# RWKV scan and expert router: a chunk's 96 rows on partitions 16 to 111, one transfer where there were two

## The chip, the core and the metric

The kernel runs on one core of a Trainium2 chip. The metric is the time of one execution in device microseconds, as the median of several runs. The profile that is shown is one execution under the hardware profiler.

## The reference, cut to what matters

Two parts follow one another. The first is a linear recurrence for each of 4 batches and 8 heads over 768 tokens of width 48. The second sends every token with a positive score through one of 8 experts.

```
state = 0                                     # 48 x 48 per batch and head
for t in range(768):
    cur = outer(u * k[t], v[t])
    y[t] = r[t] @ (state + cur)
    state = w[t][:, None] * state + outer(k[t], v[t])
x = y, laid out as 3072 tokens of 384
out = x
for the tokens with x @ w_skip > 0:
    e = argmax(x @ w_gate)
    out = x + prob[e] * (relu(x @ w1[e]) @ w2[e])
```

## The kernel before

The recurrence is done in 24 chunks of 128 tokens (4 batches of 6 chunks). A chunk's r, k and w lie in one SBUF tile `wrk`, its v transposed in a tile `vt`, and v with the tokens on the partitions in a tile `v`. A partition of `wrk` and `vt` is one of the 48 elements of one head; the four pairs of heads (`NP` = 4) lie side by side along the row. The first head of a pair has partitions 0 to 47, the second 64 to 111, and the rows from 48 to 63 and from 112 on are zeros, set once. `wrk` has three buffers, `vt` four, `v` four.

For every chunk the work goes through these steps. `products` (POOL) multiplies neighbouring decays into `p` (L281), makes `rk` = r * k (L283; for chunk 0 VectorE does it) and changes half of r and k in place (L290). `prep_scan`, `prep_keys` and `prep_reads` run the scans on VectorE (L297, L315), make `kq` on POOL (L313) and `rp` on VectorE (L320). `scores` (TensorE, L338) writes the two score matrices of a pair to `psA`, `mask` (VectorE, L354) makes `asb` of them, `keys` transposes `kq` (L347), `bonus_sums` (L363) and `bonus` (VectorE, L367) start `psY`. One step later `update` (L376) adds k-transposed times v to the state `psu`, `outputs` (L403, L408) adds the masked scores and the old state to `psY`, and `rows_out` (L421) turns the result into rows of tokens and router logits. A chunk of a batch's end has no `update`, so there are 20 of them. Three chunks are in flight at a time: while TensorE is at chunk s for `update` and `outputs`, it is at s + 1 for `scores`, and POOL is at s + 3 for `products`.

The order of the instructions on each engine is the order in which this code is written (`manual_schedule`). The loads of a chunk are issued on SP four steps ahead, by `load_chunk` (L154 for r, k, w, L156 for vt) and `load_v` (L161). Chunk 0 alone comes from an array `wrk0` whose gaps are already filled with zeros on the host, in whole transfers of 128 partitions, on SP and on ACT's queue (L146 to L151).

One more thing sets when a transfer is issued. The framework gives the transfers of SP and ACT, in order, to eight semaphores, DMAHW0 to DMAHW7, in turn. A transfer that takes a semaphore which is in use waits on its queue until the transfer that had it before has landed, and what stands behind it on that queue waits too.

At the end of the recurrence the tokens are gathered by expert, and the experts run one after the other; that part is not touched by the change.

Of the kernel before, what the change touches and what calls it, by code (L numbers as in the profile page):

```python
# [8 lines left out]
F32 = mybir.dt.float32  # L9
# [17 lines left out]
NP = H // 2  # L27
# [14 lines left out]
R_OFF = 1 + NP * CW  # L42
K_OFF = R_OFF + NP * P
V_OFF = K_OFF + NP * P
HP = 64
LO = HP + D
XW = 2 * D + E + 1
X2 = XW + 2 * D
BIG = 65536.0
# [2 lines left out]
C_ID, C_TRI, C_IOTA, C_TOK, C_DESC, C_HS = 0, 128, 256, 512, 560, 608  # L52
# [5 lines left out]
def rwkv_moe_kernel(ctx, tc, wrk, wrk0, vN, uP, wgs, wgp, w12, cst, out):  # L58
    nc = tc.nc
    dram = ctx.enter_context(tc.tile_pool(name="dram", bufs=1, space=bass.MemoryType.DRAM))  # L60
    yd = dram.tile([DM, NT], F32, name="yd")

    keep = ctx.enter_context(tc.tile_pool(name="keep", bufs=1))
# [70 lines left out]
    with tc.tile_pool(name="att", bufs=2) as att, \  # L134
# [1 line left out]
        NBUF = 3  # L136
        wrk_sb = [pers.tile([P, V_OFF], F32, name=f"wrk{i}") for i in range(NBUF)]
        vt_sb = [pers.tile([P, NP, P], F32, name=f"vt{i}") for i in range(NBUF + 1)]
        v_sb = {}

        def load_chunk(i):
            b, c = seq[i]
            t = wrk_sb[i % NBUF]
            vf = vt_sb[i % (NBUF + 1)].rearrange("p a j -> p (a j)")
            if i == 0:
                nc.sync.dma_start(t[:, :R_OFF], wrk0[:, :R_OFF])  # L146
                nc.scalar.dma_start(t[:, K_OFF:V_OFF], wrk0[:, K_OFF:V_OFF])
                nc.sync.dma_start(t[:, R_OFF:K_OFF], wrk0[:, R_OFF:K_OFF])
                nc.scalar.dma_start(c_sb[:, :C_IOTA], cst[:, :C_IOTA])
                nc.sync.dma_start(u_sb, uP)  # L150
                nc.scalar.dma_start(vf, wrk0[:, V_OFF:V_OFF + NP * P])  # L151
                return
            for g in range(2):
                nc.sync.dma_start(t[64 * g:64 * g + D], wrk[b, c, g, :, :V_OFF])  # L154
            for g in range(2):
                nc.sync.dma_start(vf[64 * g:64 * g + D], wrk[b, c, g, :, V_OFF:V_OFF + NP * P])  # L156

        def load_v(i):
            b, c = seq[i]
            v_sb[i] = att.tile([P, H, D], F32, tag="v", name=f"v{i}", bufs=4)  # L160
            nc.sync.dma_start(v_sb[i], vN[b, c])  # L161

        bias_lo = keep.tile([P, 1], F32, name="bias_lo")
        bias_hi = keep.tile([P, 1], F32, name="bias_hi")
# [9 lines left out]
        identb = keep.tile([P, P], BF16, name="identb")  # L174
        tok = c_sb[:, C_TOK:C_TOK + 2 * B * NC].rearrange("p (c q) -> p c q", q=2)
        desc = c_sb[:, C_DESC:C_DESC + NC * E].rearrange("p (c e) -> p c e", e=E)
        rows1 = c_sb[:, C_HS + 2:C_HS + 3]
        rows1_ = c_sb[:, C_HS + 3:C_HS + 4]
        wgp_sb = keep.tile([P, NP, XW], F32, name="wgp_sb")
        wgs_sb = keep.tile([P, KC, E + 1], F32, name="wgs_sb")  # L180
# [6 lines left out]
        psu = psr[:, :NP * HP].rearrange("p (a j) -> p a j", a=NP)  # L187
        psy = ps1.tile([P, NP, P], F32, tag="psY", name="psY")
        psa = [ps1.tile([P, NP, P], F32, tag=f"psA{g}", name=f"psA{g}") for g in range(2)]
        sblk = [pers.tile([P, NP, 2, HP], F32, name=f"sblk{i}") for i in range(2)]  # L190
        ohs = keep.tile([P, 1, E], BF16, name="ohs")
        key = keep.tile([P, NC, E + 1], F32, name="key")
        rall = keep.tile([P, B * NC, 1], F32, name="rall")
# [25 lines left out]

        def setup():  # L220
            load_chunk(0)
            load_v(0)
            nc.gpsimd.memset(warm, 0.0)
            nc.vector.memset(bias_lo, W_LO)
            nc.vector.memset(wrk_sb[1], 0.0)
            nc.vector.memset(bias_hi, -Q_MAX)
            nc.vector.memset(smaskb, Q_MIN)
            nc.vector.memset(smaskb.rearrange("p (a j) -> p a j", a=NP)[:, :, 0:1], 1.0)
            nc.vector.tensor_copy(pss[:, :NP * HW // 2], smaskb.bitcast(F32))
            for g in range(2):  # L230
# [38 lines left out]
        work, lgs, gens = {}, {}, {}  # L269
# [99 lines left out]
        def update(i):  # L369
            b, c = seq[i]  # L370
            if c == NC - 1:
                nc.vector.memset(psu, 0.0)
                return
            for a in range(NP):
                for g in range(2):
                    nc.tensor.matmul(psu[64 * g:64 * g + D, a, :D],  # L376
                                     work[i]["kt"][:, a, 64 * g:64 * g + D],
                                     v_sb[i][:, 2 * a + g, :D],
                                     start=False, stop=True, skip_group_check=True)

        def carry(i):
# [7 lines left out]
        def carry_out(i):  # L389
            b, c = seq[i]  # L390
            if c == NC - 1:
                return
            nb = sblk[(i + 1) % 2]
            for g in range(2):
                rows = slice(64 * g, 64 * g + HP)
                nc.scalar.copy(nb[rows, :, g, :D], psu[rows, :, :D])

        def outputs(i):
            b, c = seq[i]
            wk, v = work[i], v_sb.pop(i)  # L400
# [198 lines left out]

        with tc.manual_schedule():  # L600
            setup()
            fill(FILL0)
            products(0)
            for s in range(-2, n + 1):
                on = lambda i: 0 <= i < n
                if s + 4 < n:
                    load_chunk(s + 4)
                if on(s + 3) and s + 3 >= 1:
                    load_v(s + 3)
                if s == -2:  # L610
# [14 lines left out]
                if on(s):  # L625
                    update(s)
# [3 lines left out]
                if on(s):  # L630
                    outputs(s)
# [20 lines left out]
                if on(s):  # L652
                    carry_out(s)
# [177 lines left out]

    rv = nc.values_load(flag_i[0:1, 0:1], min_val=0, max_val=2)
    with tc.If(rv > 0):
        general_path(tc, wrk, w12, yd, u_sb, c_sb, wgs_sb, out)


def general_path(tc, wrk, w12, yd, u_sb, c_sb, wgs_sb, out):
    nc = tc.nc
    ident = c_sb[:, C_ID:C_ID + P]
    desc = c_sb[:, C_DESC:C_DESC + E]  # L840
# [2 lines left out]
    with tc.tile_pool(name="ga", bufs=1) as ga, tc.tile_pool(name="gp", bufs=2, space=PSUM) as gp:  # L843
        rt = ga.tile([P, S], F32, name="g_r")
        kt = ga.tile([P, S], F32, name="g_k")
# [35 lines left out]
    with tc.tile_pool(name="gm", bufs=1) as gm, tc.tile_pool(name="gq", bufs=1, space=PSUM) as gq:  # L881
        with tc.For_i(0, NT, P) as t0:
# [28 lines left out]
            for e in range(E):  # L911
# [77 lines left out]
```

## Time and profile before

| what | value |
|---|---|
| median of 3 runs | 312.46 us (312.44 to 315.95) |
| the profiled execution: time | 312.3 us |
| the profiled execution: span | 310.5 us |
| TensorE busy | 290.5 us (94%) |
| POOL busy | 161.5 us (52%), nearly all of it in the first 140 us |
| VectorE busy | 225.2 us (73%) |
| ScalarE busy | 153.3 us (49%) |
| bytes moved | 60.44 MB, mean 195 GB/s |

The time of an execution is its span and some 1.8 us around it. An instruction's line is that of the kernel before, as L376. "PEld" is TensorE's loading of weights, which has rows of its own and may lie beside matmuls. A float32 matmul is recorded as two instructions, so the 8 matmuls of an `update` are 16 rows. "DMA share" is the time of the packets as a share of what 16 DMA engines have; it can pass 1, since an engine may have more than one packet under way. "To landing" is the time from the start of a transfer's issue until its semaphore tells that it is there.

### The profile page before, as it was taken

What the parts mean: (1) busy time and instruction counts of PE and PEld (TensorE: products, weight loads), DVE (VectorE), ACT (ScalarE), POOL (GpSimd) and SP (SyncE); (2) the same over time, 40 slices, a digit from 0 to 9 for tenths busy, and PEclk for the clock granted to TensorE, in tenths of its full rate; (3) what the DMA queues carried; (4) which work ended last, traced back from release to release, by engine and by line L of the source; (5) the groups of instructions that cost most, each with busy time, mean ns of one, the idle gap of its engine ahead of it and who ended that gap; (6) DMA issues with size and microseconds to landing.
All of it is one profiled execution on the core that took longest, in us unless ns stands there. A gap on an engine that the chain in (4) does not pass through costs nothing.

```text
span 310.5 us, 8353 instructions
## 1 busy us (share of the span) xinstructions
PE 290.5 (94%) x3229; PEld 270.9 (87%) x3229; DVE 225.2 (73%) x486; ACT 153.3 (49%) x408; POOL 161.5 (52%) x160
## 2 busy tenths in 40 slices
PE   6589999899999999899999999999999999999990
PEld 2479898798898979789888999999999999999990
DVE  5567777999989999998553778594967859495310
ACT  3234465566356556546332648281846648282300
POOL 9897889898889999877004412221212222201111
PEclk9759999999999999999999999999999999999997
DMA  7999999999999999985111396747386774720000
GB/s 228 212 228 245 204 257 270 280 245 245 240 282 253 250 260 222 231 221 163 53 51 54 96 364 242 265 128 288 135 266 232 244 255 153 264 88 25 8 28 14
DMA packets 23777, 60.44 MB, mean 195 GB/s; under 512 B 4902, under 2 KB 11338, under 8 KB 23728
## 3 DMA queue, kind: packets, MB, share of 16 engines
q1 hardware_dynamic: 21248, 53.69, 64.0%
q0 software_dynamic: 2048, 5.48, 5.4%
q8 instruction: 27, 0.44, 0.7%
q10 hardware_dynamic: 432, 0.66, 0.6%
q14 instruction: 22, 0.18, 0.2%
HBM read 52.76 MB, written 7.86 MB: 195 GB/s over the span
## 4 chain that ended last, share of the span: by engine, by line
PE 81%; DMA 7%; DVE 6%; issue 2%; POOL 1%; ACT 1%; POOLq 0%; SPq 0%; DVEq 0%
PE psY L403 7%; PE psY L408 7%; PE psA L338 7%; PE psO L805 7%; PE psO L807 7%; PE psO L806 7%; PE psH L784 6%; PE psH L783 6%; PE psH L782 6%; PE psB L363 6%; DMA wrk<-wrk 5%; PE psX L421 5%; PE psT L347 3%; DVE asb L354 2%; PE psu L376 2%
## 5 line engine op out<-in xcount | busy, mean ns | idle before, releaser
L746 POOL DMA_INDIRECT out<-fin,ids x16 | 17.1, 1070 | 76.7 <-DVE fin L812 36.0
L789 ACT ACTIVATE hh<-psH 128x256 fp32r<-128x256 f32 x60 | 23.1, 384 | 57.1 <-PE psH L784 53.9
L784 PE MATMUL psH<-xTh,w1l 128*128 128x256 f32 x168 | 47.5, 283 | 0.0
L783 PE MATMUL psH<-xTl,w1h 128*128 128x256 f32 x168 | 47.5, 283 | 0.0
L782 PE MATMUL psH<-xTh,w1h 128*128 128x256 f32 x168 | 47.5, 283 | 0.0
L684 POOL DMA_INDIRECT xg<-out,idr x15 | 16.1, 1071 | 48.0 <-DMA out<-fin,ids 26.7
L805 PE MATMUL psO<-w2h,hh 128*128 128x384 f32 x120 | 40.7, 339 | 0.0
L807 PE MATMUL psO<-w2h,hl 128*128 128x384 f32 x120 | 40.1, 334 | 0.0
L806 PE MATMUL psO<-w2l,hh 128*128 128x384 f32 x120 | 40.1, 334 | 0.0
L290 POOL TENSOR_TENSOR wrk<-wrk 128x512 f32<-128x512 f32 x24 | 36.2, 1508 | 1.8
L413 ACT COPY xT<-psY 128x512 f32<-128x512 f32 x24 | 14.1, 586 | 45.6 <-PE psY L408 34.5
L354 DVE TENSOR_TENSOR asb<-psA,c_sb 128x512 f32<-128x512 f32 x48 | 30.7, 680 | 7.8 <-PE psA L338 7.8
L790 DVE SCALAR_TENSOR_TENSOR hl<-psH,hh 128x256 fp32r<-128x256 f32 x60 | 25.2, 420 | 12.5 <-ACT hh L789 12.1
L313 POOL TENSOR_TENSOR kq<-wrk,q 128x512 f32<-128x512 f32 x24 | 26.9, 1119 | 13.6 <-DVE q L297 12.1
L784 PEld LDWEIGHTS psH<-xTh,w1l 128*128 128x128 f32 x168 | 32.2, 192 | 0.0
L783 PEld LDWEIGHTS psH<-xTl,w1h 128*128 128x128 f32 x168 | 32.2, 192 | 0.0
L782 PEld LDWEIGHTS psH<-xTh,w1h 128*128 128x128 f32 x168 | 32.2, 191 | 0.0
L403 PE MATMUL psY<-asb,v 128*48 128x128 f32 x384 | 26.4, 281 | 5.4 <-DVE psY L367 5.3
L338 PE MATMUL psA<-rp,kq 64*64 64x128 f32 (+1 forms) x768 | 27.9, 265 | 3.1 <-POOL kq L313 3.1
L812 DVE SCALAR_TENSOR_TENSOR fin<-psO,gates,xg 128x384 f32<-128x384 f32 x15 | 9.3, 618 | 28.5 <-PE psO L807 28.5
L283 POOL TENSOR_TENSOR rk<-wrk 128x512 f32<-128x512 f32 x23 | 29.5, 1282 | 0.0
L97 DVE TENSOR_TENSOR w2l<-r,w2h 128x512 fp32r<-128x512 f32 x42 | 27.8, 687 | 1.0
(143 smaller groups left out, 680.2 us busy)
## 6 DMA issues: line engine op xcount, KB each, us to landing
r<-w SPq DMA_DIRECT2D x48, 512.0 KB, 6.0
wrk<-wrk SPq DMA_DIRECT2D x46, 288.9 KB, 7.1
v<-vN SPq DMA_DIRECT2D x24, 192.0 KB, 5.8
out<-x SPq DMA_DIRECT2D x24, 192.0 KB, 5.4
vt<-wrk SPq DMA_DIRECT2D x46, 96.0 KB, 6.1
wrk<-wrk SPq DMA_DIRECT2D x1, 258.5 KB, 3.9
wrk<-wrk ACTq DMA_DIRECT2D x1, 256.0 KB, 4.1
wrk<-wrk SPq DMA_DIRECT2D x1, 256.0 KB, 4.5
```

What stands on the lines that cost most here:

```text
L97: (eng or nc.vector).tensor_tensor(dst_l, src, dst_h.bitcast(F32), op=ALU.subtract)
L283: (nc.gpsimd if i else nc.vector).tensor_tensor(rk.rearrange("p a j -> p (a j)"), t[:, R_OFF:K_OFF], t[:, K_OFF:V_OFF], op=ALU.mult)
L290: nc.gpsimd.tensor_tensor(rk1, rk1, two(1, 1, CW), op=ALU.mult)
L338: nc.tensor.matmul(psa[g][j:j + HP, a, j:], wk["kq"][rows, a, j:j + HP], wk["rp"][rows, a, j:], start=True, stop=True)
L354: nc.vector.tensor_tensor(s, psa[g], tri.rearrange("p (o j) -> p o j", o=1).to_broadcast([P, NP, P]), op=ALU.mult)
L403: nc.tensor.matmul(psy[64 * g:64 * g + D, a], v[:, 2 * a + g], wk["asb"][g][:, a], start=False, stop=(c == 0), skip_group_check=True)
L782: nc.tensor.matmul(ps, w1h[:, o:o + P], xTh[:, kc], start=(kc == 0), stop=False)
L783: nc.tensor.matmul(ps, w1h[:, o:o + P], xTl[:, kc], start=False, stop=False)
L784: nc.tensor.matmul(ps, w1l[:, o:o + P], xTh[:, kc], start=False, stop=(kc == KC - 1))
L805: nc.tensor.matmul(pso, h[j, fc][0], w2h[:, o], start=(fc == 0), stop=False)
L806: nc.tensor.matmul(pso, h[j, fc][0], w2l[:, o], start=False, stop=False)
L807: nc.tensor.matmul(pso, h[j, fc][1], w2h[:, o], start=False, stop=(fc == FC - 1))
```

## The change

The rows of a pair's two heads move together: the first head to partitions 16 to 63, the second to 64 to 111, so that 96 rows stand without a gap (`HB` = 16, `HE` = 112). `load_chunk` then needs one transfer for r, k, w and one for vt, where it had two each. What was filled with zeros at 48 to 63 is now zero at 0 to 15.

What follows from it: the first head's matmuls write partitions 0 to 63 of `psu` and `psY`, so their weights are 64 columns wide where they were 48. In `update` both heads take 64 columns of `kt`. In `outputs` the first head takes 64 columns of v: its own 48 and the 16 that stand ahead of them, so the tile of v gets 16 columns of zeros in front (`vN_sb`, `head`), and four POOL memsets at the start fill them. The arrays that come laid out for the old places (`wrk0`, `uP`, `wgp`, a column of `cst`) are put into the new ones by `shifted`, which takes three transfers (48, 64 and 16 rows) for what was one.

```
@@ load_chunk, load_v
+        vN_sb = [pers.tile([P, HB + DM], F32, name=f"vN{i}") for i in range(4)]
+        def head(i, h, w):
+            o = HB + (h + 1) * D
+            return vN_sb[i % 4][:, o - w:o]
+        def shifted(eng, dst, src):
+            for to, of, m in ((HB, 0, D), (HP, HP, HP), (0, D, HB)):
+                eng.dma_start(dst[to:to + m], src[of:of + m])
...
             if i == 0:
-                nc.sync.dma_start(t[:, :R_OFF], wrk0[:, :R_OFF])
-                nc.scalar.dma_start(t[:, K_OFF:V_OFF], wrk0[:, K_OFF:V_OFF])
-                nc.sync.dma_start(t[:, R_OFF:K_OFF], wrk0[:, R_OFF:K_OFF])
+                for q, (dst, src) in enumerate(((t[:, :R_OFF], wrk0[:, :R_OFF]),
+                                                (t[:, K_OFF:], wrk0[:, K_OFF:V_OFF]),
+                                                (t[:, R_OFF:K_OFF], wrk0[:, R_OFF:K_OFF]))):
+                    shifted((nc.sync, nc.scalar)[q % 2], dst, src)
                 nc.scalar.dma_start(c_sb[:, :C_IOTA], cst[:, :C_IOTA])
-                nc.sync.dma_start(u_sb, uP)
-                nc.scalar.dma_start(vf, wrk0[:, V_OFF:V_OFF + NP * P])
+                shifted(nc.sync, u_sb, uP)
+                shifted(nc.scalar, vf, wrk0[:, V_OFF:V_OFF + NP * P])
                 return
-            for g in range(2):
-                nc.sync.dma_start(t[64 * g:64 * g + D], wrk[b, c, g, :, :V_OFF])
-            for g in range(2):
-                nc.sync.dma_start(vf[64 * g:64 * g + D], wrk[b, c, g, :, V_OFF:V_OFF + NP * P])
+            rows = wrk[b, c].rearrange("g d j -> (g d) j")
+            nc.sync.dma_start(t[HB:HE], rows[:, :V_OFF])
+            nc.sync.dma_start(vf[HB:HE], rows[:, V_OFF:V_OFF + NP * P])
...
-            nc.sync.dma_start(v_sb[i], vN[b, c])
+            nc.sync.dma_start(vN_sb[i % 4][:, HB:], vN[b, c].rearrange("p h d -> p (h d)"))
@@ setup
             load_chunk(0)
+            for v in vN_sb:
+                nc.gpsimd.memset(v[:, :HB], 0.0)
@@ update
-                    nc.tensor.matmul(psu[64 * g:64 * g + D, a, :D],
-                                     work[i]["kt"][:, a, 64 * g:64 * g + D],
-                                     v_sb[i][:, 2 * a + g, :D],
+                    nc.tensor.matmul(psu[64 * g:64 * g + HP, a, :D],
+                                     work[i]["kt"][:, a, 64 * g:64 * g + HP],
+                                     head(i, 2 * a + g, D),
@@ carry_out
-                nc.scalar.copy(nb[rows, :, g, :D], psu[rows, :, :D])
+                nc.scalar.copy(nb[rows, :, HB + g * D:HP + g * D], psu[rows, :, :D])
@@ outputs
-                    nc.tensor.matmul(psy[64 * g:64 * g + D, a], v[:, 2 * a + g],
+                    w = (HP, D)[g]
+                    nc.tensor.matmul(psy[64 * g:64 * g + w, a], head(i, 2 * a + g, w),
@@ the loop, s == -2 and s == -1
-                    nc.sync.dma_start(wgp_sb[:, 0::2], wgp[:, 0::2])
-                    nc.sync.dma_start(wgp_sb[:, 1::2, E + 1:], wgp[:, 1::2, :2 * D])
-                    nc.sync.dma_start(wgp_sb[:, 1::2, :E + 1], wgp[:, 1::2, 2 * D:])
+                    shifted(nc.sync, wgp_sb[:, 0::2], wgp[:, 0::2])
+                    shifted(nc.sync, wgp_sb[:, 1::2, E + 1:], wgp[:, 1::2, :2 * D])
+                    shifted(nc.sync, wgp_sb[:, 1::2, :E + 1], wgp[:, 1::2, 2 * D:])
...
+                    shifted(nc.sync, rows1, cst[:, C_HS + 2:C_HS + 3])
```

The first place is the head of SP's queue, before: chunk 0 (`wrk_83`), u, v, and chunk 1 (`wrk_84`, `vt_87`). What stands in brackets is what the issue waits for.

```order
L146 DMA wrk_83<-wrk 128x517
L148 DMA wrk_83<-wrk 128x512
L150 DMA u_sb<-uP 128x4
L161 DMA v_125<-vN 128x384
L154 DMA wrk_84<-wrk 48x1541 [waits DVE_49]
L154 DMA wrk_84<-wrk 48x1541 [waits DMAHW0_49]
L156 DMA vt_87<-wrk 48x512 [waits DMAHW1_49,Pool_49]
```

The same queue with the change (line numbers are those of the changed kernel: L148 is `shifted`, L164 and L165 the loads of a chunk, L169 that of v):

```order
L148 DMA wrk_83<-wrk 48x517
L148 DMA wrk_83<-wrk 64x517
L148 DMA wrk_83<-wrk 16x517
L148 DMA wrk_83<-wrk 48x512
L148 DMA wrk_83<-wrk 64x512 [waits DMAHW1_49]
L148 DMA wrk_83<-wrk 16x512 [waits DMAHW3_49]
L148 DMA u_sb<-uP 48x4 [waits DMAHW5_49]
L148 DMA u_sb<-uP 64x4 [waits DMAHW6_49]
L148 DMA u_sb<-uP 16x4 [waits DMAHW7_49]
L169 DMA vN_90<-vN 128x384 [waits DMAHW0_49]
L164 DMA wrk_84<-wrk 96x1541 [waits DMAHW1_49,DVE_49]
L165 DMA vt_87<-wrk 96x512 [waits DMAHW2_49,Pool_49]
```

Four transfers stood ahead of chunk 1's on SP before, ten stand there now, and from the fifth on each waits for an earlier one's landing: r's 64 rows for w's first piece, r's 16 rows for w's second, and chunk 1 for r's 64 rows.

The second place is TensorE at chunk 0's `update` and `outputs`, before:

```order
L376 MATMUL psu<-v_125,kt_249 48x48 x8
L403 MATMUL psY<-asb_0_240,v_125 48x128
L403 MATMUL psY<-asb_0_242,v_125 48x128 x2
L403 MATMUL psY<-asb_0_240,v_125 48x128 x2
L403 MATMUL psY<-asb_0_242,v_125 48x128 x2
```

and with the change:

```order
L386 MATMUL psu<-vN_90,kt_268 64x48 x8
L414 MATMUL psY<-asb_0_259,vN_90 64x128
L414 MATMUL psY<-asb_0_261,vN_90 48x128 x2
L414 MATMUL psY<-asb_0_259,vN_90 64x128 x2
L414 MATMUL psY<-asb_0_261,vN_90 48x128 x2
```

Number and order of the matmuls stay; the eight of `update` and the first head's four of `outputs` have 64 columns of weights for 48.

## Rows read from the trace of the kernel before

**Rows 1.** The page's second part: the span in 40 equal slices of 7.8 us; granted TensorE clock in tenths, DMA busy share in tenths.

```profile
PEclk9759999999999999999999999999999999999997
DMA  7999999999999999985111396747386774720000
```

**Rows 2.** Busy time by stretch (us from the span's start): length, then each engine's busy time, granted clock as a share of full speed, DMA share, GB/s.

```profile
10.00:20.00 10.00, 7.23 (x104) 6.29 (x98) 6.52 (x12) 2.76 (x7) 8.94 (x9) 0.67 1.05 220
24.00:156.00 132.00, 127.40 (x2019) 114.02 (x2019) 114.21 (x257) 73.09 (x227) 107.07 (x99) 1.00 0.94 230
160.00:310.00 150.00, 142.62 (x1041) 141.44 (x1039) 95.14 (x195) 71.01 (x157) 33.18 (x31) 0.99 0.48 164
```

The columns of engines are PE, PEld, DVE, ACT, POOL.

**Rows 3.** The chain of work that ended last, at the start: start us, us, what.

```profile
0.75 4.09 DMA wrk<-wrk
4.85 5.91 DMA wrk<-wrk
...
10.83 0.62 POOL p L281
...
12.75 1.51 POOL wrk L290
...
14.89 1.28 DVE asb L354 x2
...
16.84 1.95 PE psY L403 x16
```

**Rows 4.** The same chain over one step of the recurrence.

```profile
28.14 0.89 PE psB L363 x8
29.03 0.87 PE psX L421 x8
29.91 0.49 PE psu L376 x16
30.40 0.88 PE psY L403 x16
31.28 1.09 PE psY L408 x8
32.36 1.02 PE psA L338 x24
33.38 0.59 PE psT L347 x4
```

**Rows 5.** Who waited for whom from 24 to 156 us, of TensorE, POOL and VectorE: us in total, times, longest us.

```profile
PE psY L403 <- DVE psY L367: 2.5, 5, 0.6
...
PE psu L376 <- ACT sblk L396: 1.2, 3, 0.7
...
POOL kq L313 <- DVE q L297: 12.1, 11, 1.6
...
POOL p L281 <- DMA wrk<-wrk: 0.9, 1, 0.9
...
DVE asb L354 <- PE psA L338: 7.0, 6, 2.8
```

**Rows 6.** POOL and VectorE at the start, in order of time: start us, us, instruction, idle time before it and what ended it.

```profile
5.48 0.10 POOL L242 MEMSET ohs<- 128x8 bf16 x1
...
6.92 1.48 POOL L290 TENSOR_TENSOR wrk<-wrk 128x512 f32<-128x512 f32 x1
8.49 1.12 POOL L313 TENSOR_TENSOR kq<-wrk,q 128x512 f32<-128x512 f32 x1
10.83 0.62 POOL L281 TENSOR_TENSOR p<-wrk 128x260 f32<-128x260 f32 x1 [1.23 <-DMA wrk<-wrk]
...
20.55 0.62 POOL L281 TENSOR_TENSOR p<-wrk 128x260 f32<-128x260 f32 x1 [0.41 <-DMA wrk<-wrk]
...
5.79 0.69 DVE L283 TENSOR_TENSOR rk<-wrk 128x512 f32<-128x512 f32 x1 [1.43 <-DMA wrk<-wrk]
```

**Rows 7.** Issues of transfers on SP and ACT's queue at the start: start us, us of issuing.

```profile
1.19 0.42 SPq L148 DMA_DIRECT2D wrk<-wrk  x1
...
0.75 0.40 ACTq L147 DMA_DIRECT2D wrk<-wrk  x1
1.18 0.45 ACTq L149 DMA_DIRECT2D c_sb<-cst  x1
```

**Rows 8.** Transfers by tile: queue, number, KB each, median us from issue to landing; the last line is of L154 alone, the loads of 48 rows of r, k, w.

```profile
wrk<-wrk SPq DMA_DIRECT2D x46, 288.9 KB, 7.1
...
wrk<-wrk SPq DMA_DIRECT2D x1, 258.5 KB, 3.9
...
u_sb<-uP SPq DMA_DIRECT2D x1, 2.0 KB, 4.4
...
xg<-out,id POOLq DMA_INDIRECT x1, 3.3
...
DMA to landing us min/median/max: 4.1/7.1/8.5
```

**Rows 9.** Weight loads and a matmul by shape, from 25 to 45 us: number, busy us, mean ns of one.

```profile
L338 PEld LDWEIGHTS psA<-rp,kq 64*64 64x64 f32 x128 | 3.4, 132 | 0.5
...
L421 PEld LDWEIGHTS psX<-wgp_sb,xT 128*128 128x128 f32 x24 | 2.9, 192 | 0.0
...
L376 PEld LDWEIGHTS psu<-v,kt 128*48 128x48 f32 x48 | 1.3, 124 | 0.3
...
L421 PE MATMUL psX<-wgp_sb,xT 128*128 128x105 f32 x24 | 3.1, 273 | 0.0
```

More of the change, by code (lines that the diff above doesn't have):

```diff
@@ L45 @@
 HP = 64
-LO = HP + D
+HB = HP - D
+HE = HP + D
 XW = 2 * D + E + 1
@@ L138, in rwkv_moe_kernel @@
         vt_sb = [pers.tile([P, NP, P], F32, name=f"vt{i}") for i in range(NBUF + 1)]
-        v_sb = {}
+        vN_sb = [pers.tile([P, HB + DM], F32, name=f"vN{i}") for i in range(4)]
[5 more added lines that the diff above has]
+                eng.dma_start(dst[to:to + m], src[of:of + m])
         def load_chunk(i):
@@ L145, in load_chunk @@
             if i == 0:
-                nc.sync.dma_start(t[:, :R_OFF], wrk0[:, :R_OFF])
-                nc.scalar.dma_start(t[:, K_OFF:V_OFF], wrk0[:, K_OFF:V_OFF])
-                nc.sync.dma_start(t[:, R_OFF:K_OFF], wrk0[:, R_OFF:K_OFF])
+                for q, (dst, src) in enumerate(((t[:, :R_OFF], wrk0[:, :R_OFF]),
+                                                (t[:, K_OFF:], wrk0[:, K_OFF:V_OFF]),
+                                                (t[:, R_OFF:K_OFF], wrk0[:, R_OFF:K_OFF]))):
+                    shifted((nc.sync, nc.scalar)[q % 2], dst, src)
                 nc.scalar.dma_start(c_sb[:, :C_IOTA], cst[:, :C_IOTA])
-                nc.sync.dma_start(u_sb, uP)
-                nc.scalar.dma_start(vf, wrk0[:, V_OFF:V_OFF + NP * P])
+                shifted(nc.sync, u_sb, uP)
+                shifted(nc.scalar, vf, wrk0[:, V_OFF:V_OFF + NP * P])
                 return
-            for g in range(2):
-                nc.sync.dma_start(t[64 * g:64 * g + D], wrk[b, c, g, :, :V_OFF])
-            for g in range(2):
-                nc.sync.dma_start(vf[64 * g:64 * g + D], wrk[b, c, g, :, V_OFF:V_OFF + NP * P])
+            rows = wrk[b, c].rearrange("g d j -> (g d) j")
+            nc.sync.dma_start(t[HB:HE], rows[:, :V_OFF])
+            nc.sync.dma_start(vf[HB:HE], rows[:, V_OFF:V_OFF + NP * P])
         def load_v(i):
             b, c = seq[i]
-            v_sb[i] = att.tile([P, H, D], F32, tag="v", name=f"v{i}", bufs=4)
-            nc.sync.dma_start(v_sb[i], vN[b, c])
+            nc.sync.dma_start(vN_sb[i % 4][:, HB:], vN[b, c].rearrange("p h d -> p (h d)"))
         bias_lo = keep.tile([P, 1], F32, name="bias_lo")
@@ L176, in rwkv_moe_kernel @@
         desc = c_sb[:, C_DESC:C_DESC + NC * E].rearrange("p (c e) -> p c e", e=E)
-        rows1 = c_sb[:, C_HS + 2:C_HS + 3]
+        rows1 = keep.tile([P, 1], F32, name="rows1")
         rows1_ = c_sb[:, C_HS + 3:C_HS + 4]
@@ L189, in rwkv_moe_kernel @@
         psa = [ps1.tile([P, NP, P], F32, tag=f"psA{g}", name=f"psA{g}") for g in range(2)]
-        sblk = [pers.tile([P, NP, 2, HP], F32, name=f"sblk{i}") for i in range(2)]
+        sblk = [pers.tile([P, NP, P], F32, name=f"sblk{i}") for i in range(2)]
         ohs = keep.tile([P, 1, E], BF16, name="ohs")
@@ L395, in carry_out @@
                 rows = slice(64 * g, 64 * g + HP)
-                nc.scalar.copy(nb[rows, :, g, :D], psu[rows, :, :D])
+                nc.scalar.copy(nb[rows, :, HB + g * D:HP + g * D], psu[rows, :, :D])
         def outputs(i):
             b, c = seq[i]
-            wk, v = work[i], v_sb.pop(i)
+            wk = work[i]
             for a in range(NP):
                 for g in ((0, 1), (1, 0))[a % 2]:
-                    nc.tensor.matmul(psy[64 * g:64 * g + D, a], v[:, 2 * a + g],
+                    w = (HP, D)[g]
+                    nc.tensor.matmul(psy[64 * g:64 * g + w, a], head(i, 2 * a + g, w),
                                      wk["asb"][g][:, a], start=False, stop=(c == 0),
@@ L833, in rwkv_moe_kernel, with general_path @@
     with tc.If(rv > 0):
-        general_path(tc, wrk, w12, yd, u_sb, c_sb, wgs_sb, out)
-def general_path(tc, wrk, w12, yd, u_sb, c_sb, wgs_sb, out):
+        general_path(tc, wrk, w12, yd, uP, c_sb, wgs_sb, out)
+def general_path(tc, wrk, w12, yd, uP, c_sb, wgs_sb, out):
     nc = tc.nc
@@ L850, in general_path @@
         ev = ga.tile([2, S], F32, name="g_e")
+        u_sb = ga.tile([P, NP], F32, name="g_u")
+        nc.sync.dma_start(u_sb, uP)
         for t in (rt, kt, wt, vt, sc):
```

## The prediction

> **What bounds the kernel now.** I read the granted clock and the DMA line over the span first [rows 1], then busy time by stretch [rows 2], then the chain of waits at the start and over one step [rows 3, 4], and last the waits and the transfers at the places that the change touches [rows 5 to 9].
>
> The slices show a first part, to about 140 us, in which the transfers' line stands at 9 or more, and an expert part that the change leaves alone [rows 1]. The busy DMA line suggests that the recurrence waits for its loads. It doesn't. From 24 to 156 us TensorE is busy 127.4 of 132 us at full clock [rows 2], and one step of the chain goes from matmul to matmul without a gap: L363 0.89, L421 0.87, L376 0.49, L403 0.88, L408 1.09, L338 1.02, L347 0.59, together 5.83 us [rows 4]. POOL waited for a load of r, k, w once in that stretch, for 0.9 us; it waited 12.1 us for VectorE's scan, and VectorE 7.0 us for TensorE's scores [rows 5]. So transfers are busy but, in the steady part, early. TensorE sets the pace, with VectorE (114.2 of 132 us) and POOL (107.1) close behind it [rows 2].
>
> The start is another matter. There the chain is two transfers, the second of them half of chunk 1, issued at 4.85 and landed 5.91 us later; then POOL's p and L290, VectorE's mask, and TensorE's L403 at 16.84 [rows 3]. POOL had been idle 1.23 us for that load [rows 6]. From 16.84 us on TensorE goes from one step into the next, so a shift of this start is a shift of what follows.
>
> **The change, part by part.**
>
> *Loads of 96 rows, steady part.* Two issues fewer for each of 23 chunks, and the same bytes. From 24 to 156 us the engines of DMA moved 230 GB/s at a share of 0.94, which is 245 GB/s per full share; in the expert part, where the weights go to all 128 partitions, 164 at 0.48, which is 342 [rows 2]. So a packet of the recurrence takes longer per byte, and I expect the share to fall, to about 0.94 x 245/342 = 0.67 if all of it recovers. [...] What the end gains is another thing: only waits for loads can go, and they are 0.9 us in the steady part and 0.41 us at 20.55 [rows 5, 6], 1.3 us together. Bounds: 0 and -1.3. I take the middle, **-0.6 us**; where these waits go, POOL's next wait is for VectorE's scan.
>
> *Wider weights in `update`.* 20 updates x 16 weight loads go from 48 columns to 64; the moving side stays at 48 columns. The width of the weights costs time where it, and not the moving side, sets the pace: L421 has 105 moving columns [rows 9] and takes 0.87/8 = 109 ns per instruction, L363 with 128 takes 0.89/8 = 111 [rows 4]; both have 128 columns of weights. That is 0.87 ns per column of weights. Loads of the two heads lie beside each other: one after the other, 16 x 48 x 0.87 ns would be 0.67 us, and L376 takes 0.49 [rows 4]. So 8 pairs x 16 columns x 0.87 ns = 0.11 us per update. Lower end: L338 loads 64 columns each time [rows 9] and takes 1.02 us for its 32, 32 ns each, against 0.49/16 = 31 for L376 now [rows 4]: 0.02 us. Upper end: in proportion to the columns, 0.49 x 64/48, +0.16 us. Times 20: 0.4 to 3.2 us. I take 0.10 x 20 = **+2.0 us**, nearer to the row that differs by the moving width alone. Some of it falls where TensorE waits anyway, 2.5 us for `psY` and 1.2 for the state's copy [rows 5]; that hides about a fifth, **-0.4 us**. The rest has no cover.
>
> [...]
>
> *Wider weights in `outputs`.* Four of eight matmuls go from 48 to 64 columns. Here 128 columns move, 0.88/16 = 55 ns per instruction [rows 4], so a pair has 110 ns, while a load of 64 columns by the price above takes 56 beside its neighbour's. Nothing, hidden by the moving side; if that cover failed, 8 loads x 14 ns x 24 chunks = 2.7 us.
>
> *The start.* Four more memsets on POOL, 0.10 us each [rows 6], stand ahead of work that ends before r arrives: nothing, at most 0.4. ACT's queue gets seven transfers for three; at 0.45 us each [rows 7] its table load starts 1.8 us later, still ahead of u's landing. On SP each of chunk 0's pieces takes a semaphore, and there are eight. So r's 64 rows wait for w's first piece, and chunk 1 for r's 64 rows: three landings in a row. Before, r went out at 1.19 us [rows 7] and VectorE used it at 5.79 [rows 6]. A landing of a piece is not in the trace. Its nearest rows are the quickest gather (3.3 us) and the whole w (3.9) [rows 8]; I take 3.5, since a piece is smaller than w. Then w's first piece lands at 0.75 + 3.5 = 4.25, r's 64 rows at 7.75, and chunk 1 at 7.75 + 4.1 = 11.85, with 4.1 the quickest landing of 48 rows [rows 8], since these two halves now run together and little stands ahead of them. Chunk 0 shifts too: r's last 16 rows go out when w's second piece has landed, at 1.2 + 3.5 = 4.7, and land at 8.2; VectorE's 0.69 us [rows 6] puts L290 at 8.9 instead of 6.92, and POOL is through `kq` at 8.9 + 1.48 + 1.12 = 11.5. So chunk 1's p starts at 11.85 instead of 10.83: **+1.0 us**. Lower end -1.2, since no more than POOL's 1.23 us of idle time is to be had [rows 6]; upper end with 4.4 us a piece, as the 2 KB of u took behind these transfers [rows 8]: 0.75 + 4.4 + 4.4 + 4.1 = 13.65, +2.8.
>
> *The other pieces.* wgp's nine transfers and three of rows1 stand ahead of chunk 3 and 4 on SP. Eight more issues at 0.45 us are 3.6 us, and two fewer per chunk give 1.8 of these back by chunk 2; chunk 3's load must wait for its buffer anyway. Nothing; the wait of 0.41 us at 20.55 would grow if that cover went.
>
> **Sum.** The profiled execution took 312.3 us, 0.16 under the median of the runs. 312.3 - 0.6 + 2.0 - 0.4 + 1.0 = **314.3 us**.
>
> [...] The three runs before reach from 312.44 to 315.95.
>
> **The rivals.**
>
> *The relief pays.* The pieces land early, chunk 1 too, and the widths cost their least. 312.3 - 1.2 - 1.3 + 0.4 = 310.2 us; if all of TensorE's gaps from 24 to 156 us (132 - 127.4 = 4.6) went instead of the 1.3, it would be 306.9. For it: the slow bytes [rows 2]. Against: hardly anybody waits for them [rows 5]. Chance 0.20.
>
> *Loads in a row.* Weight loads don't pair at 64 columns: 16 x 16 x 0.87 ns = 0.22 us per update, 4.4 in 20, and with the start 312.3 + 4.4 + 1.0 - 0.6 = 317.1 us. [...] Against it stands L376's 0.49 us. Chance 0.10.
>
> *The chain of semaphores is slow.* Slower than before: if each of the three landings took the 5.91 us that chunk 1 took [rows 3], chunk 1 would come at 0.75 + 3 x 5.91 = 18.5, 7.7 us later, and the time be 312.3 + 7.7 + 1.6 = 321.6 us. It decides from landings of 5.0 us on, where the start alone costs 4.9. For: landings under load take 7.1 in the median [rows 8]. Against: at the start little is queued. Chance 0.08.
>
> *It doesn't do what it says.* 96 rows in one transfer land when the second half did before. The share stays at 0.94, the -0.6 and the early chunk 1 are gone: about 316 us. Chance 0.07.
>
> **The numbers.** The forecast has 0.55: 314.3, its own range 312 to 317. About 2% (6.2 us) is what a measurement of this kernel tells from no change: under 306.2 or over 318.7. Faster needs all gaps to close: 0.04. Slower is the slow chain, and a lost stretch of clock on top of loads in a row: 0.09. Within 2%: 0.87. The range takes the relief's 310.2 less most of a stretch of clock, and loads in a row with one: 309 to 318.5.
>
> **What would show it.** Right: a DMA share near 0.67 from 24 to 156 us; L376 at about 0.6 us in the chain and L403 still at 0.88; chunk 1's p on POOL between 11.5 and 12.5 us; no wait of POOL for `wrk` after that. Wrong: L376 unchanged (then -1.6 us), the first p of chunk 1 before 10.8 or after 14, or a DMA share that stays.

## The result and the profile after

The changed kernel took 313.79 us (median of 9 runs, 312.91 to 315.28), the kernel before 312.58 in the same comparison: a ratio of **1.0056, with an interval of 1.0028 to 1.0083**. It is slower by about 1.8 us, within the 2% that count as no change. The forecast was 314.3. Ratios here and below leave out the runs that lie more than 1.5% above the fastest of their kernel (of the kernel before three of nine here), so they can differ from the quotient of the medians. The profiled execution took 313.94 us, its span 312.1.

The lines of `before` have moved by about ten: `update` is L386 now, `outputs` L414 and L419, scores L348, keys L357, bonus L373, rows_out L432, p L291, L300 the former L290, the scan L307, kq L323. The loads of a chunk are L164 and L165, `shifted` is L148, v is L169.

Busy time by stretch, as in [rows 2], in the same columns:

```profile
10.00:20.00 10.00, 5.74 (x70) 5.17 (x72) 6.92 (x14) 2.27 (x7) 8.71 (x10) 0.67 0.81 204
24.00:156.00 132.00, 128.81 (x2010) 116.00 (x2008) 114.18 (x258) 73.18 (x227) 110.62 (x102) 1.00 0.86 236
160.00:310.00 150.00, 144.46 (x1057) 143.29 (x1055) 96.17 (x200) 71.97 (x161) 33.74 (x31) 1.00 0.48 164
```

The recurrence's DMA share fell from 0.94 to 0.86 at about the same GB/s. TensorE is busy 1.4 us more of the 132, and the expert part is as before. From 10 to 20 us TensorE did less (5.74 us against 7.23).

One step in the chain of waits, as in [rows 4]:

```profile
28.85 0.59 PE psT L357 x4
29.44 0.89 PE psB L373 x8
30.33 0.88 PE psX L432 x8
31.21 0.60 PE psu L386 x16
31.81 0.88 PE psY L414 x15
32.69 1.09 PE psY L419 x8
33.78 1.02 PE psA L348 x24
```

L386 went from 0.49 to 0.60, and nothing else moved by more than 0.01. The step is 5.95 us for 5.83.

Who waited for whom from 24 to 156 us, as in [rows 5]:

```profile
POOL kq L323 <- DVE q L307: 8.9, 7, 1.8
...
DVE asb L364 <- PE psA L348: 6.2, 5, 2.6
...
POOL p L291 <- DMA wrk<-wrk: 2.6, 1, 2.6
PE psY L414 <- DVE psY L377: 2.0, 5, 0.5
...
PE psu L386 <- ACT sblk L406: 0.6, 1, 0.6
```

Two waits of TensorE shrank from 2.5 and 1.2 us to 2.0 and 0.6. POOL's wait for a load did not go: it is 2.6 us now, in one piece.

POOL's p of the first four chunks, in order of time, as in [rows 6]:

```profile
8.22 0.62 POOL L291 TENSOR_TENSOR p<-wrk 128x260 f32<-128x260 f32 x1 [2.38 <-DMA u_sb<-uP]
...
13.21 0.62 POOL L291 TENSOR_TENSOR p<-wrk 128x260 f32<-128x260 f32 x1 [1.06 <-DMA wrk<-wrk]
...
17.90 0.62 POOL L291 TENSOR_TENSOR p<-wrk 128x260 f32<-128x260 f32 x1
...
25.16 0.62 POOL L291 TENSOR_TENSOR p<-wrk 128x260 f32<-128x260 f32 x1 [2.65 <-DMA wrk<-wrk]
```

Chunk 1's p comes at 13.21 instead of 10.83, 2.4 us later, and chunk 3's waits 2.65 us. SP's queue says why; start us and us of issuing:

```profile
0.75 5.11 SPq L148 DMA_DIRECT2D wrk<-wrk  x6
6.15 1.45 SPq L148 DMA_DIRECT2D u_sb<-uP  x3
7.64 0.42 SPq L169 DMA_DIRECT2D vN<-vN  x1
8.19 0.35 SPq L164 DMA_DIRECT2D wrk<-wrk  x1
...
11.21 8.12 SPq L148 DMA_DIRECT2D wgp_sb<-wgp  x9
19.50 0.45 SPq L164 DMA_DIRECT2D wrk<-wrk  x1
```

SP issues its transfers in the order of its queue, and each of the later pieces waits for an earlier one's landing: the six pieces of r and w took it 5.11 us, u's three 1.45. Chunk 1's load went out at 8.19; before, its second half went out at 4.85 [rows 3]. The nine pieces of wgp held SP for 8.1 us, so that chunk 3's load left at 19.50; before, it left at 14.65:

```profile
14.65 0.81 SPq L154 DMA_DIRECT2D wrk<-wrk  x2
```

Next is VectorE in the changed kernel, in order of time. It shows why chunk 1's p delays chunk 0: VectorE's order has chunk 1's scan and rp ahead of chunk 0's mask (`asb`).

```profile
13.86 0.70 DVE L307 TENSOR_TENSOR_SCAN q<-p,pss 128x260 f32<-128x260 f32 x1 [1.63 <-POOL p L291]
...
16.66 0.69 DVE L330 TENSOR_TENSOR rp<-wrk,pss 128x512 f32<-128x512 f32 x1 [1.15 <-POOL wrk L300]
17.27 1.28 DVE L364 TENSOR_TENSOR asb<-psA,c_sb 128x512 f32<-128x512 f32 x2
```

The mask starts at 17.27 instead of 14.89 [rows 3], and TensorE's first outputs at 19.21 instead of 16.84: the same 2.4 us. By the second update (25.26 us in the chain, 24.07 before) only 1.2 us of it is left, because the keys behind these outputs, and most of the bonus sums, ran at the lower clock before, and not after. The changed kernel's TensorE, in order of time:

```profile
19.21 1.80 PE L414 MATMUL psY<-asb,vN 128*64 128x128 f32 x16 [2.06 <-DVE psY L377]
...
22.84 0.66 PE L357 MATMUL psT<-c_sb,kq 128*128 128x128 f32 x4
```

and the same keys of the kernel before:

```profile
20.62 1.11 PE L347 MATMUL psT<-c_sb,kq 128*128 128x128 f32 x4
```

By stretch, in the changed kernel:

```profile
19.50:22.80 3.30, 3.30 (x48) 2.67 (x43) 2.09 (x5) 1.38 (x4) 2.86 (x3) 0.50 0.72 176
22.90:24.00 1.10, 1.10 (x12) 1.10 (x11) 1.03 (x2) 0.47 (x1) 0.00 (x0) 1.00 0.97 232
```

The granted clock was 0.50 from 19.5 to 22.8 us and 1.00 behind it, and in the kernel before it was 0.50 and 1.00 in the same two stretches. So the later kernel had less work left to run at 0.50. From there the lag grows by the wider update's 0.11 us a step, to 1.53 us at the fifth update (41.57 and 43.10 us in the chains), and then stays between 1.6 and 1.8 us: at the end it is 310.5 against 312.1 us.

### The profile page after: what moved, and what is told of

Read it like the earlier page. It is cut to its first block, busy times and chain, and to the rows that moved or that the text cites. A ratio compares the mean times of both kernels' runs of the same rounds, so it can differ in the third digit from the quotient of the medians.

```text
span 312.1 us, 8288 instructions
## 1 busy us (share of the span) xinstructions
PE 291.8 (93%) x3229; PEld 272.7 (87%) x3229; DVE 225.1 (72%) x486; ACT 153.4 (49%) x408; POOL 162.0 (52%) x164
## 4 chain that ended last, share of the span: by engine, by line
PE 83%; DVE 7%; DMA 5%; issue 1%; ACT 1%; SPq 0%; POOL 0%; POOLq 0%; DVEq 0%
PE psA L348 7%; PE psY L414 7%; PE psY L419 7%; PE psO L819 7%; PE psO L817 7%; PE psO L818 7%; PE psH L796 6%; PE psH L795 6%; PE psH L794 6%; PE psB L373 6%; PE psX L432 5%; PE psH L128 4%; PE psT L357 3%; DVE asb L364 2%; PE psu L386 2%; DMA vt<-wrk 2%
## 5 line engine op out<-in xcount | busy, mean ns | idle before, releaser
L696 POOL DMA_INDIRECT xg<-out,idr x15 | 17.0, 1131 | 47.8 <-DMA out<-fin,ids 27.4
L300 POOL TENSOR_TENSOR wrk<-wrk 128x512 f32<-128x512 f32 x24 | 36.2, 1510 | 2.4 <-DVE rk L293 0.6
L802 DVE SCALAR_TENSOR_TENSOR hl<-psH,hh 128x256 fp32r<-128x256 f32 x60 | 25.2, 420 | 12.5 <-ACT hh L801 12.2
L348 PE MATMUL psA<-rp,kq 64*64 64x128 f32 (+1 forms) x768 | 27.9, 265 | 5.5 <-POOL kq L323 5.5
L323 POOL TENSOR_TENSOR kq<-wrk,q 128x512 f32<-128x512 f32 x24 | 26.9, 1121 | 11.6 <-DVE q L307 8.9
L414 PE MATMUL psY<-asb,vN 128*64 128x128 f32 (+1 forms) x384 | 26.3, 281 | 4.2 <-DVE psY L377 4.1
L348 PEld LDWEIGHTS psA<-rp,kq 64*64 64x64 f32 x768 | 21.8, 139 | 8.8 <-POOL kq L323 6.0
```

The costliest lines, as they stand in the source:

```text
L300: nc.gpsimd.tensor_tensor(rk1, rk1, two(1, 1, CW), op=ALU.mult)
L323: nc.gpsimd.tensor_tensor(pairs(kq), pairs(wk["k"]), twice(wk["q"][:, :, 1:HW]), op=ALU.mult)
L348: nc.tensor.matmul(psa[g][j:j + HP, a, j:], wk["kq"][rows, a, j:j + HP], wk["rp"][rows, a, j:], start=True, stop=True)
L414: nc.tensor.matmul(psy[64 * g:64 * g + w, a], head(i, 2 * a + g, w), wk["asb"][g][:, a], start=False, stop=(c == 0), skip_group_check=True)
```

## The experiments

The parts of the change pull in different ways, so each was done alone or undone. Ratios are to the kernel before in the same comparison; 0.01 is 3.1 us.

**1. The change without pieces.** The host lays the first chunk, u, wgp and rows1 out for the new places, so that each goes in whole.

```diff
...
-                    shifted((nc.sync, nc.scalar)[q % 2], dst, src)
+                nc.sync.dma_start(t[:, :R_OFF], wrk0[:, :R_OFF])
+                nc.scalar.dma_start(t[:, K_OFF:V_OFF], wrk0[:, K_OFF:V_OFF])
+                nc.sync.dma_start(t[:, R_OFF:K_OFF], wrk0[:, R_OFF:K_OFF])
...
-                shifted(nc.sync, u_sb, uP)
+                nc.sync.dma_start(u_sb, uPs)
...
-                    shifted(nc.sync, wgp_sb[:, 0::2], wgp[:, 0::2])
+                    nc.sync.dma_start(wgp_sb[:, 0::2], wgp[:, 0::2])
...
```

> The change, but the host lays wrk0, uP, wgp and the column rows1 out for the new places, so that each is one transfer again where the change took three. Theory (the pieces cost the start, the wider weights hardly count, and one transfer for two brings little): chunk 1's p on POOL starts at 10.8 us or earlier instead of 13.2, POOL's wait of 2.65 us for chunk 3 goes, and the time is 312.5 us, 1.3 under the change and level with before. Rival 1 (the pieces are hidden and the wider weights make all of the 1.2 us): it stays at 313.8. Rival 2 (one transfer gains much and the start hid it): 310.5 or less.

Measured: 309.1 us (308.65 to 311.6, 12 runs), **0.9929 [0.9896, 0.9961]**: 4.0 us less than the change by the ratios (1.0056 - 0.9929). The theory's 312.5, only 1.3 us below the change, was far off, and its rival 2 came true: the pieces cost three times that. Experiment 4, the change but for a narrower weight load, ran in the same comparison and lies 0.0133 above. By stretch:

```profile
0.00:24.00 24.00, 18.99 (x216) 14.24 (x217) 17.10 (x35) 9.09 (x24) 22.93 (x36) 0.86 0.95 266
24.00:156.00 132.00, 128.44 (x1970) 115.59 (x1969) 111.61 (x255) 72.87 (x228) 105.63 (x98) 1.00 0.80 223
```

Its chunk 1, on SP and then on POOL:

```profile
2.59 0.63 SPq L163 DMA_DIRECT2D wrk<-wrk  x1
```

```profile
9.65 0.62 POOL L290 TENSOR_TENSOR p<-wrk 128x260 f32<-128x260 f32 x1
```

The load goes out at 2.59, and p runs at 9.65 without waiting for a load, as do all later ones. This is the lower end of the prediction's start, and it beats both kernels.

**2. The loads of experiment 1 in two again**, to partitions 16 to 63 and 64 to 111; all else as in 1.

```diff
-            nc.sync.dma_start(t[HB:HE], rows[:, :V_OFF])
+            for g in range(2):
+                nc.sync.dma_start(t[HB + D * g:HP + D * g], rows[D * g:D * g + D, :V_OFF])
...
```

> As e1, but each chunk's r, k, w come in two transfers of 48 rows (partitions 16 to 63 and 64 to 111), and vt too: the one thing for which the change was made is undone alone. Theory (no wait for loads is on the path in the steady part): at most 0.5 us over e1, DMA share from 24 to 156 us back at 0.94 or above. Rival 2 (one transfer gains much): 1.5 us or more over e1.

Measured: 312.62 us, 1.0028 [0.9992, 1.0063]. One transfer for two is worth 3.1 us by the ratios (3.5 by the medians), which is rival 2 and not the theory's 0.5. By stretch:

```profile
0.00:24.00 24.00, 16.76 (x142) 12.13 (x142) 14.55 (x29) 7.34 (x18) 20.60 (x34) 0.79 0.96 215
24.00:156.00 132.00, 128.61 (x2012) 115.61 (x2011) 114.12 (x258) 73.08 (x227) 107.95 (x100) 1.00 0.93 231
```

The granted clock from 0 to 24 us is 0.79 against 0.86, the share from 24 to 156 us 0.93 against 0.80. In the chains of these two profiled executions the second update starts at 24.27 against 20.12 us, and the span ends at 311.2 against 307.2: all of the difference is made by then. The landing itself is the smaller part of it, since chunk 1's p starts at 11.04 against 9.65. With two loads TensorE was idle 2.77 us ahead of the first outputs, and the granted clock behind that was 0.50 (17.0 to 22.5 us); with one it was idle 0.19 us, and the clock was 1.00 from 15.5 us on. The two outputs, experiment 1 ahead:

```profile
15.66 1.09 PE L413 MATMUL psY<-asb,vN 128*64 128x128 f32 x16 [0.19 <-DVE psY L376]
```

```profile
17.05 1.97 PE L415 MATMUL psY<-asb,vN 128*64 128x128 f32 x16 [2.77 <-DVE psY L378]
```

**3. The wider update alone**, in the kernel before.

```diff
-                    nc.tensor.matmul(psu[64 * g:64 * g + D, a, :D],
-                                     work[i]["kt"][:, a, 64 * g:64 * g + D],
+                    nc.tensor.matmul(psu[64 * g:64 * g + HP, a, :D],
+                                     work[i]["kt"][:, a, 64 * g:64 * g + HP],
```

> The kernel before, with the update's weights 64 columns wide for 48 and nothing else. Both theories: 0.60 us per update in the chain instead of 0.49. Theory (VectorE's pace takes up most of it): +0.4 to +0.8 us, so 313.0 to 313.4 beside 312.5. Rival 1 (the width is on the path in all 20 updates): +2.0 us, 314.5.

Measured: 313.14 us, 0.9986 [0.9939, 1.0033]. In the chain the update takes the 0.60 us that were priced:

```profile
27.33 0.60 PE psu L376 x16
```

The interval, though, takes in everything from a gain of 1.9 to a loss of 1.0 us. It is inconclusive on what the end pays. Its profiled execution also had another clock at the start, 0.86 over the first 24 us against 0.79 before. It came to the second update 2.8 us ahead of the kernel before (21.26 and 24.07) and yet ended 1.2 us behind it (311.7 and 310.5): a lead at the start need not last.

**4. The second head's weights of the update back to 48 columns**, in the changed kernel.

```diff
+                    w = (HP, D)[g]
-                    nc.tensor.matmul(psu[64 * g:64 * g + HP, a, :D],
+                    nc.tensor.matmul(psu[64 * g:64 * g + w, a, :D],
```

> The change, with the second head's weights in the update 48 columns wide again; the first head keeps 64. Theory (the loads of a pair lie beside each other, so the wider one sets the pace): still 0.60 us per update, and the time of the change, 313.8. Rival (loads one after the other): half of the 0.11 us goes, 0.55 us per update; on the path in 20 updates that would be 1.1 us less, 312.7.

Measured: 313.64 us, 1.0062 [1.0031, 1.0092], the same as the change. Update and outputs in its chain (it counts 13 of the update's 16 rows, the last of which lie among the first of the outputs):

```profile
37.02 0.54 PE psu L387 x13
37.55 0.95 PE psY L415 x16
```

Together they take 1.48 us, as in the changed kernel (0.60 + 0.88); without half of the 0.11 us it would be 1.43. Half of the added columns are gone and nothing came back, as the theory has it for two heads' loads that lie beside each other, the wider of which sets the pace.

**5. Loads alone**, in four ways one after the other: two of 48 rows to 0 to 47 and 64 to 111, one of 96 to 16 to 111, one of 128, two of 48 to 16 to 63 and 64 to 111.

```diff
+                nc.sync.dma_start(ta[i % NB][64 * g:64 * g + D], flat[r:r + D, :V_OFF])
...
+            nc.sync.dma_start(ta[i % NB][16:112], flat[96 * i:96 * i + 96, :V_OFF])
...
+            nc.sync.dma_start(ta[i % NB], flat[P * i:P * i + P, :V_OFF])
...
+                nc.sync.dma_start(ta[i % NB][16 + D * g:64 + D * g], flat[r:r + D, :V_OFF])
```

> Nothing of the computation is done: the kernel loads the 24 chunks' r, k, w (14.2 MB) four times over, one stage after the other, and writes zeros. Stage 1: two transfers of 48 rows, to partitions 0 to 47 and 64 to 111; stage 2: one of 96 rows to 16 to 111; stage 3: one of 128 rows for as many bytes; stage 4: two of 48 rows, to 16 to 63 and 64 to 111. [...]

Measured, in the page's slices of 6.7 us (one execution):

```profile
DMA  4999999999999999999999999899999999999998
GB/s 92 181 184 185 190 184 187 180 188 182 192 183 253 275 278 275 281 277 281 284 418 418 417 418 393 151 166 169 163 168 168 168 166 166 168 168 168 160 390 304
```

The DMA line stands at 9 throughout, while the rate goes from about 185 GB/s to 278, 418 and 167. So in this run a full DMA line says nothing about speed. One transfer of 96 rows moves 1.5 times what two of 48 do (278 GB/s for 185), and 0.67 of what one of 128 rows does (418).

**6. wgp and rows1 whole**, in the changed kernel; the first chunk, u and v stay in pieces.

```diff
-                    shifted(nc.sync, wgp_sb[:, 0::2], wgp[:, 0::2])
+                    nc.sync.dma_start(wgp_sb[:, 0::2], wgp[:, 0::2])
...
```

> The change, with wgp and rows1 whole again (3 transfers for 12 on SP) and chunk 0 and u still in pieces. If chunk 0's pieces make the loss: POOL's wait of 2.65 us for chunk 3 goes, but the time stays within 0.7 us of the change, 313.1 to 313.8. If wgp's nine pieces make it: 310.5 or less.

Measured: 312.73 us, 1.0034 [1.0001, 1.0066], 0.7 us below the change by the ratios, 1.1 by the medians. Chunk 1's p and chunk 3's, on POOL:

```profile
12.93 0.62 POOL L291 TENSOR_TENSOR p<-wrk 128x260 f32<-128x260 f32 x1 [0.32 <-DMA wrk<-wrk]
...
22.20 0.62 POOL L291 TENSOR_TENSOR p<-wrk 128x260 f32<-128x260 f32 x1
```

Chunk 3's wait of 2.65 us is gone, and chunk 1 is nearly as late as in the change. So the pieces of wgp and rows1 cost 0.7 to 1.1 us, somewhat more than expected; the intervals overlap, so this is not clear of noise. The pieces of the first chunk and u make the other 3.3 (1.0034 - 0.9929), and there the intervals don't meet.

**7 and 8. Experiments 1 and 2 with the clock held up**: 14 more warm-up matmuls at the start, and 14 ahead of the first outputs. They write nothing that is read, but they take time of TensorE, so the clock is not all that they change.

```diff
-FILL0 = 12
+FILL0 = 26
...
+                if s == 0:
+                    fill(14)
                 if on(s):
                     outputs(s)
```

> e1 with 28 more warm-up matmuls on zeros, 14 ahead of the first scores and 14 ahead of the first outputs, where TensorE was idle, so that its clock need not fall. If part of e1's gain over e3 is the clock: the granted clock stays at full speed through 24 us in both, and e7 and e8 lie 1.0 to 1.6 us apart (chunk 1's earlier landing alone) instead of 3.5. e7 itself 0 to 1.5 us under e1.

> e3 with the same 28 matmuls. By the same theory 2 to 3 us under e3 (309.6 to 310.6). Rival: what e3 loses is the landings alone and not the clock; then it stays at 312 to 313.

Measured: 309.07 us, 0.9911 [0.9883, 0.994], with one transfer; 311.22, 0.9986 [0.9952, 1.002], with two. The first stretch of each, experiment 7 ahead:

```profile
0.00:24.00 24.00, 21.93 (x243) 14.25 (x244) 16.97 (x34) 8.93 (x23) 22.93 (x36) 1.00 0.95 257
```

```profile
0.00:24.00 24.00, 21.42 (x225) 13.69 (x228) 16.12 (x32) 8.03 (x22) 20.98 (x34) 1.00 0.95 227
```

The granted clock is 1.00 in both, and 2.3 us are left between them (0.0075), more than the 1.0 to 1.6 expected: the intervals don't meet. Experiment 8 itself lies above its 309.6 to 310.6. At the second update (20.40 and 21.08 us in the chains) the difference is 0.7 us, at the end 1.7 (307.2 and 308.9). In between, POOL waited for loads in the kernel with two transfers, and not at all in the other. Its waits from 0 to 156 us in experiment 8:

```profile
POOL p L292 <- DMA wrk<-wrk: 2.6, 4, 1.1
```

**9 and 10. The kernel before with the same warm-up matmuls, and with the wider update on top.** The edits are those of experiments 7 and 3.

> The kernel before with the same 28 warm-up matmuls, so that the clock at the start does not tell the runs apart. Theory (before loses 1 to 2 us to the clock at its start): 310.0 to 311.3, full clock through 24 us.

> The same with the update's weights 64 columns wide: the price of the width by itself, without the clock's part in e2. Theory (of 20 x 0.11 = 2.2 us most falls where VectorE sets the pace): 0.4 to 0.9 us over e9. Rival (all on the path): 2.0 to 2.2 us over e9.

Measured: 312.01 us, 0.9968 [0.9931, 1.0005], and 312.68, 1.0012 [0.9976, 1.0048]. The wider update cost 0.7 us by the medians and 1.4 by the ratios, and the spans of the profiled executions are 1.6 apart (309.3 and 310.9). That lies between the 0.4 to 0.9 expected and the rival's 2.0 to 2.2, and the intervals overlap. Experiment 9 lies above its 310.0 to 311.3: the kernel before gained 1.0 us with its clock at 1.00, and the interval takes in no gain at all. With its two loads POOL then waited more, 4.4 us from 0 to 156 us instead of 2.7. Experiment 9, and the kernel before behind it:

```profile
POOL p L281 <- DMA wrk<-wrk: 4.4, 6, 1.1
```

```profile
POOL p L281 <- DMA wrk<-wrk: 2.7, 4, 1.2
```

**The parts together**, by ratios: two loads and the wider update at the new places cost 0.0028 over the kernel before (experiment 2), one transfer for two gives 0.0099, and the pieces take 0.0127: 0.9, -3.1 and +4.0 us. They add to the 1.8 us measured because each is taken from the one before it; the 0.9 by itself is not clear of noise.

**From the second update to the last.** The chains of the profiled executions, one of each kernel, show when two loads are enough. First and last line of the stretch, for experiment 1 (one load), experiment 8 (two) and the kernel before (two):

```profile
20.12 0.60 PE psu L385 x16
...
145.53 0.67 PE psu L385 x16
```

```profile
21.08 0.60 PE psu L387 x16
...
147.35 0.67 PE psu L387 x16
```

```profile
24.07 0.49 PE psu L376 x16
...
148.75 0.49 PE psu L376 x16
```

With one load the stretch takes 125.3 to 125.4 us, wherever it starts from 20.1 to 25.3 us (the change, experiments 1, 6 and 7). With two it takes 124.7 and 125.5 where it starts at 24.1 and 24.3 (the kernel before and experiment 2), but 126.3 to 128.9 where it starts at 21.1 to 21.4 (experiments 3, 8, 9 and 10). So two loads keep up with a start as late as that of the kernel before, and fall behind one that is about 3 us earlier. Experiment 4 is an exception with one load, 126.8 us from 23.7 us on: wgp's pieces make chunk 3 late there too, and the start is not late enough to hide it.

## Why the prediction was right, and where its terms were not

The time and the forecast case held. In the two profiled executions the change stood 1.2 us behind at the second update, where the forecast had +1.0 for the start, and lost 0.4 us more from there to the end, where it had +1.0 (+2.0, -0.4 and -0.6). That the total came so near is in part luck: both are what is left of larger parts that pull against each other, the pieces' +4.0 and the single transfer's -3.1 us, and the working had neither at that size. Of the signs that were to show it right, L386's 0.60 and L414's 0.88 us held; the DMA share, the time of chunk 1's p and "no wait of POOL for `wrk`" did not.

- **Start: +1.0 us, measured +2.4 at chunk 1's p and +1.2 at the second update.** The p at 13.21 lies outside the 11.5 to 12.5 forecast, inside the upper end (13.65); the clock then gave half of it back, which the prediction had in the range alone. The chain of semaphores was the right mechanism, but the working followed only r's 64 rows. On SP's queue, behind r's last 16 rows, stood u's three pieces, each waiting for a landing, and v, so chunk 1 went out at 8.19 and not at 7.75, and its p started 5.0 us later and not 4.1. Chunk 0's p was late too, after 2.38 us of waiting at 8.22: its operand reaches one column into r's columns, so by the code it needs the pieces of r as well as those of w. (The profile puts this wait down to u, which p does not read.) The rival of slow landings was not needed: the pieces at the start that show a landing took 2.1 to 4.3 us, where 3.5 was priced. A few more landings in the row did it. ACT's queue fared alike: its table load started 4.1 us later (6.28 for 2.14) and not 1.8, though nothing is seen to wait for it.
- **Other pieces: nothing, measured 0.7 to 1.1 us** (experiment 6), not clear of noise. The working priced their issues (eight more, though the code has nine) and not their waits for semaphores, 2.4 us of the 8.1 for which wgp's nine held SP. The cover named, that chunk 3's load waits for its buffer anyway, was too short: with wgp whole that load goes out at 13.64, not 19.50. The wait of 0.41 us that "would grow if that cover went" grew to 2.65.
- **Loads of 96 rows: -0.6 us in the steady part.** In the change it did not show: POOL's wait for a load there grew from 0.9 to 2.6 us. By itself one transfer was worth 3.1 us (experiments 1 and 2), all of it made by the second update. With the clock held it was worth 2.3 (7 and 8), and the profiled executions have 0.7 us at the second update and 1.0 behind it, which is inside the term's bounds of 0 and -1.3. What was wrong is that only the waits of the one profile could go. The 2.7 us that POOL waited in the kernel before are what was left after everything else had been late: with its second update 2.8 us earlier, the same two loads made POOL wait 4.4 us (experiment 9). And the start's gain was bounded by POOL's 1.23 us; it was that at p (9.65 for 10.83), but 4.0 us at the second update (20.12 for 24.07), since the clock came back earlier in the kernel's work (1.00 from 15.5 us on, where the kernel before was still at 0.50 from 19.5 to 22.8).
- **Wider update: 0.11 us each, as worked out**, 0.60 in the chain. How much of it the end pays stays open. Three comparisons (experiments 3; 2 against before; 10 against 9) give -0.4, +0.9 and +1.4 us against a net +1.6 forecast, none of them clear of noise, and the first had another clock at its start. From the second update to the last, experiment 2 takes 0.8 us more than the kernel before, experiment 10 takes 1.7 more than 9. In the change TensorE's two waits shrank by 1.1 us together, half of the 20 x 0.11 = 2.2 and not a fifth.
- **Wider outputs: nothing.** Right, 0.88 us for 0.88.
- **DMA share: 0.67 forecast, 0.86 measured**, 0.80 without the pieces. It was scaled with the 342 GB/s per full share of the experts' weights, which fill 128 partitions; 96 rows alone reach 278 (experiment 5), and 236/0.86 is 274. The price that was missing was one of 96 rows.
- **A stretch of clock, in the range and in the chance of slower alone.** No run shows the size of this term. What the runs showed in its place: the same keys took 1.11 us at a granted clock of 0.50 (the kernel before) and 0.66 at 1.00 (the change), and with the first 24 us at 1.00 the time was 0.6 to 1.3 us shorter by the ratios (experiments 7, 8 and 9), not clear of noise.

Of the rivals, *loads in a row* fell with experiment 4 and with the 0.60 us of an update, which its 0.22 us more would have made 0.71. *The relief pays* was true of the transfer by itself and was masked by the pieces: experiment 1 is its 310.2 us and a little better. *It doesn't do what it says* fell with the share and with experiment 5. *The chain of semaphores is slow* was true in kind: chunk 1's p came 2.4 us later, not 7.7.

In experiment 5 two transfers of 48 rows to 0 to 47 and 64 to 111 reached 0.44 of the rate of 128 rows (185 of 418 GB/s), and one of 96 rows to 16 to 111 reached 0.67. What sets these rates, the number of the rows or their places, no run here tells, nor why 16 to 63 and 64 to 111 (167 GB/s) were slower than 0 to 47 and 64 to 111.

Not tried: the first chunk whole with u alone in pieces, or the pieces in another order on SP. Which of them costs most of the 3.3 us is open.

## What to carry to other kernels

Price a change of layout by what it does to the start: here the transfers split in three cost issues, waits for semaphores and their place in SP's queue, 4.0 us by the ratios, and that gave back more than the 3.1 us that one transfer for two won. Laying the few one-time arrays out on the host for the new places kept the gain (309.1 us). Do not bound the worth of a faster load by the waits of one profile: the kernel before waited 2.7 us for its loads, and 4.4 to 6.4 us where its second update came 2.7 to 2.8 us earlier (experiments 3, 9 and 10). This is no rule: at the new places the waits were 3.3 us in experiment 2 and 2.6 in 8. And read GB/s beside the DMA line, which in experiment 5 was full at 167 as at 418.

## What the runs showed of the hardware that was not expected

- Two transfers of 48 rows moved 167 GB/s to partitions 16 to 63 and 64 to 111, 185 to 0 to 47 and 64 to 111; one of 96 rows 278, one of 128 rows 418. All of them at a full DMA line.
- 28 more matmuls at the start raised the granted clock of the first 24 us to 1.00. With two loads, from 0.79, the time fell by 1.3 us (experiments 2 and 8: 0.0042) and 1.0 (9); with one load, from 0.86, by 0.6 or nothing (1 and 7: 0.0018, and 309.1 against 309.07 us). None of these is clear of noise: the intervals overlap.
- Kernels with two loads scattered more: eleven of the twelve runs of experiment 2 lie from 310.67 to 314.75 us and of experiment 8 from 310.03 to 313.24, eleven of the twelve of experiment 1 from 308.65 to 309.25 and all eleven of 7 from 308.75 to 309.81.
